# A transformer block on one core: three up-projections placed at the end of attention, the output weights as half-precision parts, two buffers for the token activations

## Chip, cores and metric

One core of a Trainium2 chip. The metric is the device time of one execution in microseconds; the profiled execution is one more execution of the same program.

## The reference

2048 tokens of 448 features. Layer norm, then 16-head attention (28 features a head), an output projection `wo` and a residual; then layer norm and a product-key expert layer (PEER): 16 heads each score 64 + 64 keys, take the best 8 of each, the best 8 of their 64 sums, a softmax over these, and of 4096 experts (`u`, `v`) sum the chosen.

```python
h = x + softmax(q @ k.T * Dh ** -0.5) @ v @ wo          # q, k, v = layernorm(x) @ wqkv, per head
xf = layernorm(h)
s1, s2 = xf @ w_q[..., :dk] @ k1.T, xf @ w_q[..., dk:] @ k2.T
i1, i2 = top8(s1), top8(s2); top_s, top_e = top8(t1[:, None] + t2[None, :])
act = gelu(einsum("nd,nhkd->nhk", xf, u[top_e]))
h2 = h + einsum("nhk,nhk,nhkd->nd", softmax(top_s), act, v[top_e])
```

## The kernel before

Every product that needs more than half precision is made from parts: `products` (L50) lists 4 + 4 + 3 matmuls of high and low parts, `mm_all` (L90) issues these 11, so that all of them carry line 92. Tokens go in four blocks `b` of 512, in tiles of 128.

**First stage (to about 160 us).** Layer norm, queries, keys and values; they go to DRAM. The weights are scaled by a power of two that a `Scale` (L130) finds: `see` takes a maximum on VectorE (DVE), `share` spreads it over the partitions with a transposition on TensorE (PE), `set` computes the scale. `values_of` (L410) writes the values with a per-partition scale `vscale`.

**Attention (L550, to about 872 us).** 256 steps `u`: 16 groups `n` (4 blocks x 4 groups of 4 heads) of 16 key tiles. In each step PE makes the scores of step u + 2 (L563), ScalarE (ACT) takes exponentials (L567), PE sums the values (L589). `load_kv` (L217) loads a piece of four key tiles, keys at L212 and values at L224, in one of four buffers, into the buffer that has just been read; so a piece is issued some 11 steps before PE first reads it. `finish` (L570) transposes and normalizes a group's output into `ob`. Beside the steps a `weave` (L174) runs generators, each with a count of steps and an interval of time in steps; whichever is due first issues next. Folding the expert queries' weights and splitting `u` and `v` run there, and for blocks 0 to 2 the output projection `project(b)` (L635), the search for the best keys `search(b)` (L753), and the pairs, partly on GpSimd (POOL, L810). `load_wo` (L622) loads `wo` and splits it into two 32-bit parts that PE reads as fp32r, on DVE (L626) and POOL (L627).

**`project`, a tile of 128 tokens:** transposes of `ob` (L121), high part on ACT or DVE, low part (L127, L128), 11 matmuls with `woh` and `wol` (L92), activation to `at` (L666), residual, moments (L711, L109, L112), norm (L115), transposes and the parts `XHb`, `XLb` in `X[b]`.

**Last projection, first weights, last scores (872 to 965 us).** `project(3)` with its own buffers, `weights(0)` (L932) and `kept_scores(3)` (L731) are woven (L1119, L1134). `weights(b)` reads the chosen slots from DRAM (`st`), makes per 16 tokens a comparison `p1` (L969) and per 32 tokens factors (L948, L954) on DVE, and sums them on PE (L996) into `G`, 32 times.

**Experts (965 us to the end).** Per block 32 slices `f`: `up` (L1141) is 11 matmuls of 512 columns and a Gelu into a ring of buffers, `weigh` (L1157) multiplies by `G` (L1163), and splits (L1164, L1165), then 12 matmuls into four sums (L1190). `ready` (L1172) sets how far `up` runs ahead: before the sums of slice f, f + 3 are made or n + (32 - n)(f + 1) // 26 if that is more, n being those made before the block; block 0 starts with n = 0. Beside block 0 a generator `later` does the rest of the pairs and all searches of block 3 on DVE, transposes slots on PE (L899) and copies them on ACT (L96); it is set to run over the first 58% of the block.

DMAs are issued from SyncE's queue (SP), which takes them in order. Lines of one engine's queue mostly follow the order written, but some that are ready earlier stand ahead of others.

Of the kernel before, what the change touches and what calls it, by code (L numbers as in the profile page):

```python
# [29 lines left out]
LS = 2.0 ** 11  # L30
TOP = 14
ONE = 2.0 ** 15
QS = 2.0 ** 2 / (XS * 2.0 ** TOP)

# [26 lines left out]
def block(ctx: ExitStack, tc: tile.TileContext, x, wqk, wv, wo, wq, k12, uT, v, cst, out):  # L61
# [20 lines left out]
    gscale = const.tile([128, 1], F32)  # L82
    vscale = const.tile([128, 1], F32)
    escale = const.tile([128, 4], F32)
# [84 lines left out]
    def times(dst, src, c):  # L169
        nc.vector.tensor_scalar(dst, src, c, None, op0=OP.mult)  # L170
# [46 lines left out]
    def load_kv(n):  # L217

        if n < len(PIECES):
            _, g, c = PIECES[n]  # L220
            kS = lp.tile([128, 2, 512], F16, name="kS", bufs=4)
            halves(kS, ks_d[g], slice(512 * c, 512 * c + 512))
            V = lp.tile([128, 4, 4, 32], F32, name="V", bufs=4)
            nc.sync.dma_start(V.rearrange("p t h d -> p (t h d)"), v_d[g, c].rearrange("p t c -> p (t c)"))  # L224
            kv[n] = kS, V

# [77 lines left out]

    US, VS, WS = Scale(0, 32), Scale(1, 32), Scale(2, H)

    fp = ExitStack()
    raw_p = fp.enter_context(tc.tile_pool(name="raw", bufs=2, reuse_waits="tile"))
    with ExitStack() as c0:
# [48 lines left out]
        def scale_wv():  # L358
            S = Scale(3, 2)
            scaled(S, wvr, [(wvh[:, 2 * i:2 * i + 2], wvl[:, 2 * i:2 * i + 2]) for i in range(2)])  # L360
            times(vscale, S.floor, 2.0 ** -TOP / XS)

# [47 lines left out]
        def values_of(b):  # L410
            for j in range(4):
                c = slice(128 * j, 128 * j + 128)
                pv = ps.tile([128, D], F32, name="pq", bufs=4)
                mm_all(pv, products(lambda t: XH[b][:, t, c], lambda t: XL[b][:, t, c],
                                    lambda t: wvh[:, t], lambda t: wvl[:, t]))
                nc.scalar.activation(vst[j][:, :, :DH], pv.rearrange("p (h d) -> p h d", h=H), AF.Identity, scale=vscale)
                (nc.scalar if b > 1 else nc.sync).dma_start(v_d[:, b, :, j].rearrange("g p c -> p g c"),
                                                                    vst[j].rearrange("p (g h) d -> p g (h d)", g=4))
# [131 lines left out]
    def attention(paired):  # L550
# [32 lines left out]
        def values(u, Pt):  # L583
            n, k = divmod(u, NT)
            if k == 0:
                O[n] = P[0].tile([128, 512], F32, name="A")
            V = kv[u // 4][1]
            for j in range(4):
                nc.tensor.matmul(O[n][32 * j:32 * j + 32], V[:, k % 4, j], Pt[:, j], start=k == 0, stop=k == NT - 1)  # L589
            if k % 4 == 3:  # L590
                load_kv(u // 4 + 4)
            if k == NT - 1:
                o = pp.tile([128, 512], F32, name="o", bufs=1)
                nc.vector.tensor_copy(o, O.pop(n))  # L594
                return o
# [11 lines left out]
        for u in range(steps):  # L607
            if u + 2 < steps:
                Pts[u + 2] = scores(u + 2)
            flush()  # L610
            if u % NT == 2 and u > NT:
                finish(u // NT - 1, done)
            if u in Pts:
                summed(u)
            if u in paired:
                summed(u + 1)
            yield
        finish(4 * NB - 1, done)
        yield


    def load_wo():  # L622
        prev = None
        for g in range(5):
            if prev:
                nc.vector.tensor_copy(woh[:, g - 1], prev)  # L626
                nc.gpsimd.tensor_tensor(wol[:, g - 1], prev, woh[:, g - 1].bitcast(F32), op=OP.subtract)  # L627
            if g < 4:
                prev = w2.tile([128, 512], F32, name="wor", tag="xt")[:, :D]
                nc.sync.dma_start(prev, wo[:, g])  # L630
            yield

    X = {}

    def project(b, offset=5, room=None):  # L635

        X[b] = XH, XL = bx.tile([128, 4, 512], F16, name="XHb"), bx.tile([128, 3, 512], F16, name="XLb")

# [3 lines left out]
        def tile_of(j):  # L642
# [59 lines left out]
    def load_X(b):  # L702
        X[b] = XH, XL = bx.tile([128, 4, 512], F16, name="XHb"), bx.tile([128, 3, 512], F16, name="XLb")
        nc.sync.dma_start(XH, x_d[b][:, :4])
        nc.sync.dma_start(XL, x_d[b][:, 4:])

    def moments(pool, xt):
# [345 lines left out]
    with tc.manual_schedule(engines={ET.PE, ET.DVE, ET.Activation, ET.Pool, ET.SP}):  # L1053
        load_kv(2)
        load_kv(3)
        begin = [67 + 4, 67 + 64, 67 + 128]
        start = [t + 26 for t in begin]
# [16 lines left out]
        for k in range(8):  # L1074
            nc.gpsimd.memset(places[:, k], float(k))
        r2 = ExitStack()
# [27 lines left out]


    us = {}

    def load_u(f):
        u = be.tile([128, 2, 4, 128], F16, name="u")
        nc.sync.dma_start(u.rearrange("p k t e -> p k (t e)"), us_d[f])  # L1110
        return u

    with tc.manual_schedule(engines={ET.PE, ET.DVE, ET.Activation, ET.Pool, ET.SP}):
        room = {"xt": [ring[4 * j + 2] for j in range(4)], "at": [ring[3], ring[7]]}
        pools = [tc.tile_pool(name="sw0", bufs=1, side="right", reuse_waits="tile")]
        with ExitStack() as c1:
            pools = [c1.enter_context(pools[0])]
            w0, sc = weights(0), kept_scores(3, pools)
            weave((project(3, 2, room), 12, 0, 0.25), (islice(w0, 1), 1, 0.01, 0.02), (islice(sc, 1), 1, 0.02, 0.03),  # L1119
                  (islice(w0, 8), 8, 0.05, 0.27), (islice(sc, 4), 4, 0.125, 0.29))  # L1120
            r2.close()
            be = ctx.enter_context(tc.tile_pool(name="be", bufs=3, reuse_waits="tile"))
            c2 = c1.enter_context(ExitStack())
# [3 lines left out]
            def loads():  # L1127
                store_X(3)
                yield
                for f in range(3):  # L1130
# [7 lines left out]
    ring += [bv.tile([128, 512], F32, name=f"ring{i}", bufs=1) for i in range(16, 20)]  # L1138
    acts = {}

    def up(b, f, name):  # L1141

        XH, XL = X[b]
        u = us.pop(f, None) or load_u(f)
        p = P[0].tile([128, 512], F32, name=name)
        mm_all(p, [(l, r) for r, l in products(lambda t: XH[:, t], lambda t: XL[:, t],
                                               lambda t: u[:, 0, t], lambda t: u[:, 1, t])])
        act = ring[f % 20] if b else ring[16 + f % 4]
        nc.scalar.activation(act, p, AF.Gelu_apprx_tanh, scale=ugelu)  # L1149
        acts[f] = act  # L1150

    def ups(b, n):
# [60 lines left out]
    for b in range(NB):  # L1213
        n = AHEAD if b else 0
        if b:
# [59 lines left out]
```

## Time and profile before

| | us |
|---|---|
| median of 3 runs | 1644.02 (1638.12 to 1646.05) |
| profiled execution | 1642.62 |
| span of its profile | 1640.8 |
| PE busy | 1560.6 (95%) |
| DVE busy | 1198.4 (73%) |
| ACT busy | 931.9 (57%) |
| POOL busy | 364.7 (22%) |

Busy time counts an instruction from its start to its end; matmuls overlap, so PE can be busy for the whole of a stretch and still not run at its peak. The granted clock is TensorE's, as a share of 2.4 GHz; 0.50 is 1.2 GHz. A row of a timeline begins with the start and the length in us; what is in brackets is the engine's idle time just before and what ended it.

### The profile page before, as it was taken

What the parts mean: (1) busy time and instruction counts of PE and PEld (TensorE: products, weight loads), DVE (VectorE), ACT (ScalarE), POOL (GpSimd) and SP (SyncE); (2) the same over time, 40 slices, a digit from 0 to 9 for tenths busy, and PEclk for the clock granted to TensorE, in tenths of its full rate; (3) what the DMA queues carried; (4) which work ended last, traced back from release to release, by engine and by line L of the source; (5) the groups of instructions that cost most, each with busy time, mean ns of one, the idle gap of its engine ahead of it and who ended that gap; (6) DMA issues with size and microseconds to landing.
All of it is one profiled execution on the core that took longest, in us unless ns stands there. A gap on an engine that the chain in (4) does not pass through costs nothing.

```text
span 1640.8 us, 33316 instructions
## 1 busy us (share of the span) xinstructions
PE 1560.6 (95%) x12585; PEld 678.9 (41%) x12585; DVE 1198.4 (73%) x3875; ACT 931.9 (57%) x1272; POOL 364.7 (22%) x488
## 2 busy tenths in 40 slices
PE   5999999999999998999988998999999999999999
PEld 3444222233333332233325654455545554555444
DVE  7762432645688677765798999959999899779832
ACT  3545778979888887888773443233423344334322
POOL 1241003555204565487524000000000000000000
PEclk9999999999999999999998999999999999999999
DMA  8424965677853475457622434444444533554454
GB/s 281 134 97 129 305 215 190 213 242 253 286 173 96 151 242 180 130 162 235 189 87 78 131 94 148 125 125 144 119 127 138 156 105 108 156 153 129 117 146 129
DMA packets 158881, 263.34 MB, mean 160 GB/s; under 512 B 14336, under 2 KB 90880, under 8 KB 158720
## 3 DMA queue, kind: packets, MB, share of 16 engines
q1 hardware_dynamic: 154496, 259.12, 50.5%
q10 hardware_dynamic: 4224, 2.10, 0.4%
q8 instruction: 98, 1.61, 0.4%
q14 instruction: 63, 0.52, 0.1%
HBM read 211.88 MB, written 49.28 MB: 159 GB/s over the span
## 4 chain that ended last, share of the span: by engine, by line
PE 63%; DVE 27%; DMA 5%; ACT 2%; issue 2%; POOL 1%; SPq 0%; DVEq 0%; POOLq 0%; ACTq 0%
PE acc L1190 14%; PE M L92 12%; PE A L589 10%; PE S L563 9%; PE A L92 7%; PE pq L92 6%; DVE p L969 4%; DVE ti L799 3%; DVE pos L826 2%; DVE G L990 2%; DVE ti L798 2%; ACT P L567 2%; DVE fg L954 2%; DMA raw<-in_uT_dram 2%; PE M L262 1%
## 5 line engine op out<-in xcount | busy, mean ns | idle before, releaser
L567 ACT ACTIVATE P<-S,escale 128x1024 f32<-128x1024 f32 x512 | 534.5, 1131 | 75.9 <-PE S L563 75.9
L1190 PE MATMUL acc<-v,w 128*128 128x448 f16 x1536 | 305.4, 352 | 0.1
L589 PE MATMUL A<-P,V 128*32 128x512 f32 x2048 | 266.0, 609 | 3.7 <-DVE o L594 3.7
L563 PE MATMUL S<-qS,kS 32*128 32x512 f16 x3072 | 240.1, 380 | 7.7 <-ACT P L567 6.0
L1190 PEld LDWEIGHTS <-w 128*128 128x128 f16 x1536 | 148.7, 98 | 141.3 <-ACT w L1164 0.9
L1164 ACT ACTIVATE w<-ring 128x512 f16<-128x512 f32 x128 | 80.5, 630 | 209.7 <-PE acc L1190 109.9
L92 PEld LDWEIGHTS <-u 128*128 128x128 f16 x1408 | 133.7, 98 | 152.5 <-issue 12.3
L969 DVE TENSOR_TENSOR p<-st,iota 128x2048 f16<-128x2048 f16 x128 | 156.0, 1219 | 7.7 <-PE A L996 4.1
L563 PEld LDWEIGHTS <-kS 32*128 32x128 f16 x3072 | 65.8, 92 | 210.6 <-issue 171.7
L92 PE MATMUL A<-XHb,u 128*128 128x512 f16 x568 | 137.8, 386 | 5.1 <-DVE G L990 3.9
L1165 DVE SCALAR_TENSOR_TENSOR w<-w,ring 128x512 f16<-128x512 f16 x128 | 87.2, 687 | 66.2 <-ACT w L1164 66.2
L92 PE MATMUL M<-w,XHb 128*128 128x512 f16 x512 | 127.9, 380 | 4.2 <-DVE ob L580 3.1
L1163 DVE SCALAR_TENSOR_TENSOR ring<-ring,wscale,G 128x512 f32<-128x512 f32 x128 | 92.7, 744 | 34.6 <-ACT ring L1149 34.5
L92 PE MATMUL M<-XHb,u 128*128 128x512 f16 x456 | 112.4, 382 | 0.8 <-DVE G L990 0.8
L1149 ACT ACTIVATE ring<-A,ugelu 128x512 f32<-128x512 f32 x71 | 48.5, 684 | 84.6 <-PE A L92 84.6
L589 PEld LDWEIGHTS A<-P,V 128*32 128x32 f32 x2048 | 45.8, 109 | 119.1 <-issue 108.3
L850 POOL TENSOR_TENSOR sel<-sel,iv 128x256 f16<-128x256 f16 x80 | 54.4, 712 | 171.6 <-DVE sel L846 171.6
L798 DVE MAX8 ti<-fresh 128x8 f32<-128x64 f32 x384 | 80.6, 210 | 16.3 <-ACT fresh L776 16.2
L1149 ACT ACTIVATE ring<-M,ugelu 128x512 f32<-128x512 f32 x57 | 39.2, 688 | 81.7 <-PE M L92 81.5
L799 DVE FIND_INDEX8 ti<-ti,fresh 128x8 uint32<-128x64 f32 x384 | 84.2, 219 | 0.0
L1026 POOL TENSOR_SCALAR raw<-raw,scale 128x512 f32<-128x512 f32 (+1 forms) x64 | 47.3, 740 | 151.8 <-PE M L262 112.2
L954 DVE TENSOR_TENSOR fg<-f,st 128x2048 f16<-128x2048 f16 x64 | 78.0, 1218 | 0.1
(197 smaller groups left out, 2130.4 us busy)
## 6 DMA issues: line engine op xcount, KB each, us to landing
v<-vs SPq DMA_DIRECT2D x128, 336.0 KB, 2.9
u<-us SPq DMA_DIRECT2D x128, 256.0 KB, 2.6
w<-wp SPq DMA_DIRECT2D x56, 512.0 KB, 5.9
kS<-ks SPq DMA_DIRECT2D x64, 256.0 KB, 4.5
V<-vd SPq DMA_DIRECT2D x64, 256.0 KB, 2.8
raw<-in_uT_dram SPq DMA_DIRECT2D x64, 256.0 KB, 5.3
wr<-in_wq_dram SPq DMA_DIRECT2D x32, 448.0 KB, 4.3
raw<-in_v_dram SPq DMA_DIRECT2D x64, 224.0 KB, 5.1
```

The source lines that it names most:

```text
L92: nc.tensor.matmul(ps, l, r, start=i == 0, stop=i == len(pairs) - 1)
L563: nc.tensor.matmul(S[j // 2][:, j % 2], kS[r, a, 128 * (k % 4):128 * (k % 4) + 128], qS[r, c], start=m == 0, stop=m == 2)
L567: nc.scalar.activation(Pt[:, 2 * i:2 * i + 2], S[i], AF.Exp, scale=escale[:, n % 4:n % 4 + 1])
L589: nc.tensor.matmul(O[n][32 * j:32 * j + 32], V[:, k % 4, j], Pt[:, j], start=k == 0, stop=k == NT - 1)
L798: nc.vector.max(t8[:, 4 * i + k], src[:, 64 * k:64 * k + 64])
L799: nc.vector.max_index(i8[:, 4 * i + k], t8[:, 4 * i + k], src[:, 64 * k:64 * k + 64])
L954: nc.vector.tensor_tensor(fg.rearrange("p t k f u -> p t k (f u)"), f1.rearrange("p t f u -> p t (f u)").unsqueeze(2).to_broadcast([128, T ...
L969: newest[0] = nc.vector.tensor_tensor(p1, pairs(0, s, TG, 128), ids(TG, 128), op=OP.is_equal).ins
L1149: nc.scalar.activation(act, p, AF.Gelu_apprx_tanh, scale=ugelu)
L1163: nc.vector.scalar_tensor_tensor(av, av, wscale, of_expert(b, f), op0=OP.mult, op1=OP.mult)
L1165: nc.vector.scalar_tensor_tensor(w[:, 1], w[:, 0], -LS, a, op0=OP.mult, op1=OP.add)
L1190: nc.tensor.matmul(acc[j][:, :D], l, r, start=f == 0 and k == 0, stop=f == 31 and k == 2)
```

## The change

- `wo` is scaled by a power of two (`WO`, a `Scale`) and split into two fp16 parts, both on DVE; the attention's output is split into fp16 parts too. The values carry a fixed scale `VS1` instead of `vscale`, and a pointer scale `pscale` after the projection makes up for both. The first project starts two steps later (67 + 6 instead of 67 + 4), the search of block 2 ends two steps earlier.
- Keys and values have three buffers instead of four, a piece is issued some 7 steps before PE first reads it.
- `XHb` and `XLb` have two buffers. `X[0]`, the first three `u` slices and the slots of `weights(0)` are loaded in the last steps of the attention.
- Block 0's first three up-projections run early: `up(0, 0)` before the attention's last `finish`, in a buffer of the scores; `up(0, 1)` and `up(0, 2)` at the head of the next stage. Block 0 then starts with three made.
- The first step of `weights(0)` on DVE stands at the head of that stage, before `project(3)`.

The diff, cut to its core (`up`, `load_u` and the pool `be` move up in the file unchanged but for `p`):

```diff
-            kS = lp.tile([128, 2, 512], F16, name="kS", bufs=4)
+            kS = lp.tile([128, 2, 512], F16, name="kS", bufs=3)
...
-            V = lp.tile([128, 4, 4, 32], F32, name="V", bufs=4)
+            V = lp.tile([128, 4, 4, 32], F32, name="V", bufs=3)
...
-                nc.scalar.activation(vst[j][:, :, :DH], pv.rearrange("p (h d) -> p h d", h=H), AF.Identity, scale=vscale)
+                nc.scalar.activation(vst[j][:, :, :DH], pv.rearrange("p (h d) -> p h d", h=H), AF.Copy, scale=VS1)
...
-                load_kv(u // 4 + 4)
+                load_kv(u // 4 + 3)
...
+        up(0, 0, None, pss.tile([128, 2, 512], F32, name="S")[:, 0])
         finish(4 * NB - 1, done)
...
     def load_wo():
...
-                nc.vector.tensor_copy(woh[:, g - 1], prev)
-                nc.gpsimd.tensor_tensor(wol[:, g - 1], prev, woh[:, g - 1].bitcast(F32), op=OP.subtract)
...
+        for g, r in enumerate(raws):
+            nc.sync.dma_start(r, wo[:, g])
+        yield
+        yield
+        for g, r in enumerate(raws):
+            WO.see(g, r)
+            if g == 1:
+                yield
+        yield from WO.share()
+        yield
+        for g, r in enumerate(raws):
+            times(woh[:, g], r, WO.scale)
+            nc.vector.scalar_tensor_tensor(wol[:, g], r, WO.scale, woh[:, g], op0=OP.mult, op1=OP.subtract)
+            if g == 1:
+                yield
+        nc.vector.tensor_scalar(pscale, WO.floor, VW.floor, 2.0 ** (-TOP - 4), op0=OP.mult, op1=OP.mult)
...
-            oh = w2.tile([128, 4, 128], FR, name="oh2", bufs=1)
-            ol = w2.tile([128, 3, 128], FR, name="ol2", bufs=1)
+            oh = w2.tile([128, 4, 128], F16, name="oh2", bufs=1)
+            ol = w2.tile([128, 3, 128], F16, name="ol2", bufs=1)
...
-            nc.scalar.activation(at, pa[:, :D], AF.Copy)
+            nc.scalar.activation(at, pa[:, :D], AF.Identity, scale=pscale)
...
-        begin = [67 + 4, 67 + 64, 67 + 128]
+        begin = [67 + 6, 67 + 64, 67 + 128]
...
-        woh = wo_p.tile([128, 4, D], FR)
-        wol = wo_p.tile([128, 4, D], FR)
-        work = [(a, 257 - FOLDED, 0, 257 - FOLDED), (load_wo(), 5, 0, 5)]
+        woh = wo_p.tile([128, 4, D], F16)
+        wol = wo_p.tile([128, 4, D], F16)
+        work = [(a, 257 - FOLDED, 0, 257 - FOLDED), (load_wo(), 9, 0, 6.5)]
...
-            work += [(look, SEARCH, t, t + SEARCH)]
+            work += [(look, SEARCH, t, t + SEARCH - 2 * (b == 2))]
...
+        def first_loads():
+            load_X(0)
+            for f in range(3):
+                us[f] = load_u(f)
+                yield
+            next(w0)
+            yield
+
+        w0 = weights(0)
+        work += [(first_loads(), 5, 174, 184)]
...
-            w0, sc = weights(0), kept_scores(3, pools)
-            weave((project(3, 2, room), 12, 0, 0.25), (islice(w0, 1), 1, 0.01, 0.02), (islice(sc, 1), 1, 0.02, 0.03),
-                  (islice(w0, 8), 8, 0.05, 0.27), (islice(sc, 4), 4, 0.125, 0.29))
+            sc = kept_scores(3, pools)
+            def first_up(f):
+                up(0, f, "A")
+                yield
+
+            weave((first_up(1), 1, 0, 0), (islice(w0, 1), 1, 0, 0.002), (project(3, 2, room), 12, 0, 0.25), (first_up(2), 1, 0.012, 0.012), (islice(sc, 1), 1, 0.02, 0.03),
+                  (islice(w0, 7), 7, 0.05, 0.27), (islice(sc, 4), 4, 0.125, 0.29))
...
-            load_X(0)
...
-        n = AHEAD if b else 0
+        n = AHEAD if b else UP0
```

## Rows read from the trace of the kernel before

**Rows 1.** Stages: length, busy us of each engine (instructions), granted clock, DMA share, GB/s

```profile
335.00:870.00 535.00, 517.26 (x4611) 171.48 (x4605) 383.70 (x1905) 444.06 (x479) 264.41 (x355) 0.99 0.57 182
870.00:905.00 35.00, 27.28 (x232) 19.94 (x231) 27.59 (x57) 9.25 (x16) 16.61 (x24) 0.80 0.33 106
905.00:965.00 60.00, 56.77 (x1040) 37.98 (x1039) 55.73 (x58) 25.50 (x43) 0.22 (x1) 0.99 0.35 109
965.00:1062.00 97.00, 91.67 (x471) 44.13 (x468) 97.00 (x579) 31.02 (x51) 0.00 (x0) 0.97 0.45 133
1062.00:1131.00 69.00, 67.21 (x497) 35.69 (x496) 45.78 (x69) 24.45 (x51) 0.00 (x0) 1.00 0.45 135
```

The engines stand in the order PE, PEld (its weight loads), DVE, ACT, POOL.

**Rows 2.** The same view, five microseconds each, in the last projection

```profile
885.00:890.00 5.00, 2.29 (x42) 1.68 (x40) 4.32 (x9) 2.09 (x4) 1.85 (x3) 0.85 0.32 97
890.00:895.00 5.00, 4.45 (x11) 3.51 (x11) 4.82 (x7) 0.96 (x2) 0.01 (x1) 0.50 0.09 35
```

**Rows 3.** Timeline of PE: a projection with 32-bit parts, and what follows

```profile
366.90 1.08 PE L92 MATMUL M<-woh,oh 128*128 128x448 f32 x4
...
369.33 0.83 PE L563 MATMUL S<-qS,kS 32*128 32x512 f16 x12
```

**Rows 4.** Timeline of PE: two successive groups of the values projection

```profile
141.89 0.92 PE L92 MATMUL pq<-wvh,XH 128*128 128x448 f16 x4
...
143.97 0.92 PE L92 MATMUL pq<-wvh,XH 128*128 128x448 f16 x4
```

**Rows 5.** Timeline of DVE: the weights of slice 14 in block 0

```profile
1044.84 0.68 DVE L1165 SCALAR_TENSOR_TENSOR w<-w,ring 128x512 f16<-128x512 f16 x1
```

**Rows 6.** Waits of PE in block 0: total us, times, longest

```profile
PE M L899 <- ACT st L96: 5.2, 1, 5.2
```

**Rows 7.** Groups of instructions by line and form: busy us, mean ns

```profile
L416 ACT ACTIVATE vst<-pq,vscale 128x448 f32<-128x448 f32 x16 | 10.2, 635 | 19.9 <-PE pq L92 18.4 <-issue 1.4
L666 ACT ACTIVATE at<-M 128x448 f32<-128x448 f32 x12 | 6.5, 544 | 14.3 <-PE M L92 14.3
L1149 ACT ACT_TABLE_LOAD x3 | 3.8, 1283 | 0.1
```

**Rows 8.** Timeline of SP: the load of the 20th piece of keys

```profile
329.03 0.49 SPq L212 DMA_DIRECT2D kS<-ks  x1
```

**Rows 9.** Timeline of PE: the first scores that read this piece

```profile
351.77 1.08 PE L563 MATMUL S<-qS,kS 32*128 32x512 f16 x12
```

**Rows 10.** DMA issues: count, KB each, median us from issue to landing

```profile
kS<-ks SPq DMA_DIRECT2D x64, 256.0 KB, 4.5
```

**Rows 11.** Timeline of PE: the second and third up-projection and the first sum

```profile
968.61 1.89 PE L92 MATMUL A<-XHb,u 128*128 128x512 f16 x8
...
970.99 1.89 PE L92 MATMUL A<-XHb,u 128*128 128x512 f16 x8
...
973.36 2.73 PE L1190 MATMUL acc<-v,w 128*128 128x448 f16 x12
```

**Rows 12.** The chain that ended last: one of two equal projection groups

```profile
876.46 4.46 PE M L92 x11
```

**Rows 13.** Timeline of PE: the attention's last transposes

```profile
872.68 0.66 PE L577 MATMUL M<-ct,o 128*128 128x128 f32 x4 [1.34 <-DVE o L594]
```

**Rows 14.** Waits of DVE from 868 to 965 us

```profile
DVE f L948 <- DMA st<-sd: 2.0, 1, 2.0
DVE ring L668 <- ACT ring L666: 2.0, 1, 2.0
DVE ol L127 <- ACT oh L651: 1.2, 1, 1.2
```

**Rows 15.** Timeline of DVE: the first factors and comparison of the first weights

```profile
878.31 0.74 DVE L948 TENSOR_TENSOR f<-st,iota 128x1024 f16<-128x1024 f16 x1 [2.00 <-DMA st<-sd]
...
880.23 1.31 DVE L969 TENSOR_TENSOR p<-st,iota 128x2048 f16<-128x2048 f16 x1
```

**Rows 16.** Timeline of PE: the sums of slice 14 in block 0

```profile
1048.76 2.43 PE L1190 MATMUL acc<-v,w 128*128 128x448 f16 x12
```

More of the change, by code (lines that the diff above doesn't have):

```diff
@@ L31 @@
 TOP = 14
+UP0 = 3
 ONE = 2.0 ** 15
+VS1 = 2.0 ** 4 / (XS * 2.0 ** TOP)
 QS = 2.0 ** 2 / (XS * 2.0 ** TOP)
@@ L82, in block @@
     gscale = const.tile([128, 1], F32)
-    vscale = const.tile([128, 1], F32)
+    pscale = const.tile([128, 1], F32)
     escale = const.tile([128, 4], F32)
@@ L303, in parts @@
                 nc.sync.dma_start(wp_d[h // 4][:, :, h % 4].rearrange("p f t c -> p f (t c)"), hl)
-    US, VS, WS = Scale(0, 32), Scale(1, 32), Scale(2, H)
+    US, VS, WS, VW, WO = Scale(0, 32), Scale(1, 32), Scale(2, H), Scale(3, 2, 60), Scale(8, 4, 60)
     fp = ExitStack()
@@ L358, in scale_wv @@
         def scale_wv():
-            S = Scale(3, 2)
-            scaled(S, wvr, [(wvh[:, 2 * i:2 * i + 2], wvl[:, 2 * i:2 * i + 2]) for i in range(2)])
-            times(vscale, S.floor, 2.0 ** -TOP / XS)
+            scaled(VW, wvr, [(wvh[:, 2 * i:2 * i + 2], wvl[:, 2 * i:2 * i + 2]) for i in range(2)])
         def scale_wqk(g):
@@ L622, in load_wo @@
     def load_wo():
-        prev = None
-        for g in range(5):
-            if prev:
-                nc.vector.tensor_copy(woh[:, g - 1], prev)
-                nc.gpsimd.tensor_tensor(wol[:, g - 1], prev, woh[:, g - 1].bitcast(F32), op=OP.subtract)
[L628 to L631, printed above, removed]
+        raws = [w2.tile([128, 512], F32, name="wor", tag="xt")[:, :D] for _ in range(2)]
+        raws += [w2.tile([128, 4, 128], F32, name=n, bufs=1).rearrange("p t c -> p (t c)")[:, :D] for n in ("of", "xf")]
+        for g, r in enumerate(raws):
[15 more added lines that the diff above has]
+        yield
     X = {}
     def project(b, offset=5, room=None):
-        X[b] = XH, XL = bx.tile([128, 4, 512], F16, name="XHb"), bx.tile([128, 3, 512], F16, name="XLb")
+        X[b] = XH, XL = bx.tile([128, 4, 512], F16, name="XHb", bufs=2), bx.tile([128, 3, 512], F16, name="XLb", bufs=2)
         def place(j, name, tag, bufs):
@@ L702, in load_X, with load_u, up @@
     def load_X(b):
-        X[b] = XH, XL = bx.tile([128, 4, 512], F16, name="XHb"), bx.tile([128, 3, 512], F16, name="XLb")
+        X[b] = XH, XL = bx.tile([128, 4, 512], F16, name="XHb", bufs=2), bx.tile([128, 3, 512], F16, name="XLb", bufs=2)
         nc.sync.dma_start(XH, x_d[b][:, :4])
         nc.sync.dma_start(XL, x_d[b][:, 4:])
+    us, acts = {}, {}
+    def load_u(f):
+        u = be.tile([128, 2, 4, 128], F16, name="u")
+        nc.sync.dma_start(u.rearrange("p k t e -> p k (t e)"), us_d[f])
+        return u
+    def up(b, f, name, p=None):
+        XH, XL = X[b]
+        u = us.pop(f, None) or load_u(f)
+        if p is None:
+            p = P[0].tile([128, 512], F32, name=name)
+        mm_all(p, [(l, r) for r, l in products(lambda t: XH[:, t], lambda t: XL[:, t],
+                                               lambda t: u[:, 0, t], lambda t: u[:, 1, t])])
+        act = ring[f % 20] if b else spare[f % 4]
+        nc.scalar.activation(act, p, AF.Gelu_apprx_tanh, scale=ugelu)
+        acts[f] = act
     def moments(pool, xt):
@@ L1054, in block @@
         load_kv(2)
-        load_kv(3)
-        begin = [67 + 4, 67 + 64, 67 + 128]
+        begin = [67 + 6, 67 + 64, 67 + 128]
         start = [t + 26 for t in begin]
@@ L1075, in block @@
             nc.gpsimd.memset(places[:, k], float(k))
+        be = ctx.enter_context(tc.tile_pool(name="be", bufs=3, reuse_waits="tile"))
+        spare = [be.tile([128, 512], F32, name=f"ring{i}", bufs=1) for i in range(16, 19)]
         r2 = ExitStack()
@@ L1103, in block @@
     ring = [gp.tile([128, 512], F32, name=f"ring{i}") for i in range(16)]
[L1106 to L1111, printed above, removed]
     with tc.manual_schedule(engines={ET.PE, ET.DVE, ET.Activation, ET.Pool, ET.SP}):
@@ L1117, in block @@
             pools = [c1.enter_context(pools[0])]
-            w0, sc = weights(0), kept_scores(3, pools)
-            weave((project(3, 2, room), 12, 0, 0.25), (islice(w0, 1), 1, 0.01, 0.02), (islice(sc, 1), 1, 0.02, 0.03),
-                  (islice(w0, 8), 8, 0.05, 0.27), (islice(sc, 4), 4, 0.125, 0.29))
+            sc = kept_scores(3, pools)
+            def first_up(f):
+                up(0, f, "A")
+                yield
+            weave((first_up(1), 1, 0, 0), (islice(w0, 1), 1, 0, 0.002), (project(3, 2, room), 12, 0, 0.25), (first_up(2), 1, 0.012, 0.012), (islice(sc, 1), 1, 0.02, 0.03),
+                  (islice(w0, 7), 7, 0.05, 0.27), (islice(sc, 4), 4, 0.125, 0.29))
             r2.close()
-            be = ctx.enter_context(tc.tile_pool(name="be", bufs=3, reuse_waits="tile"))
             c2 = c1.enter_context(ExitStack())
@@ L1129, in loads @@
                 yield
-                for f in range(3):
+                for f in range(UP0, UP0 + 3):
                     us[f] = load_u(f)
@@ L1134, in block @@
             weave((w0, WEIGHTS - 9, 0.29, 1), (sc, 13, 0.29, 0.92), (loads(), 4, 0.6, 0.8))
-            load_X(0)
     bv = ctx.enter_context(tc.tile_pool(name="bv", bufs=3, reuse_waits="tile"))
     gw = ctx.enter_context(tc.tile_pool(name="gw", bufs=2, side="right", reuse_waits="tile"))
[L1138 to L1150, printed above, removed]
+    spare.append(bv.tile([128, 512], F32, name="ring19", bufs=1))
+    ring += spare
     def ups(b, n):
```

## The prediction

> **What bounds the kernel now.** I read the stages first, then who waits in each, then single stretches in order of time. The stages [rows 1] show three regimes. From 335 to 870 us (the attention's main part) the TensorE (PE) is busy 517 of 535 us and the VectorE (DVE) 384: PE sets the pace, with ScalarE (ACT, 444) close behind. From 870 to 965 us (the last projection, the first weights and the last scores) neither engine is full: PE 27.3 of 35 and 56.8 of 60, DVE 27.6 of 35 and 55.7 of 60. So this stretch is a chain between them, and PE also loses time to its clock: the granted clock is 0.80 there, and 0.50, the 1.2 GHz level, from 890 to 895 us, after five microseconds with PE busy for only 2.29 [rows 1, 2]. From 965 to 1062 us, the first two thirds of block 0 of the experts, DVE is busy 97.00 of 97 us and PE 91.7; from 1062 to 1131 us PE has 67.2 of 69 and DVE only 45.8. Block 0 is thus bound by both, one after the other. The later blocks run after 1131 us; the change doesn't touch their work, and I give them nothing.
>
> **The change, part by part.**
>
> *Half-precision output weights in attention.* A projection multiplies 11 pairs of 448 columns. With the 32-bit parts, a group takes 369.33 - 366.90 = 2.43 us from its first matmul to the next work [rows 3]. The same 11 x 448 columns with half-precision parts, in the values projection at full clock, take 143.97 - 141.89 = 2.08 us [rows 4]. That is 0.35 us less for each of 12 tiles that run inside the attention, 4.2 us. PE is the bound there, so I count it whole; the bounds are 0 (ACT takes over between projections) and 4.2.
>
> By the Trainium skill's "TensorE: Matmul & The Clock Gate", section "Back-to-back issue gap", a matmul's spacing is its columns over 2.4 GHz plus 2.5 ns, 189 ns for 448 columns whatever the type: by that the old group would take 2.08 us too, and the 4.2 us would be 0. The trace shows 221 ns (2.43 us over 11), so I go by the row; the other outcome is rival 3.
>
> *Loading wo.* Before: four casts on DVE, four subtractions on POOL. After: four reductions, a transposition of the maximum on PE, a few one-column operations, then eight scaling operations on DVE, near 0.7 us each by the nearest row [rows 5], so some 6 us more DVE work. DVE is idle 28% of this stage [rows 1], so this work is free; without that cover it would cost those 6 us. Not free is PE's wait for the transposition's input: behind it in PE's queue stand the scores of the next step, and ACT waits for these. The first project starts two steps later, and the search after it runs into the next one by a step, both inside filled PE time. Nearest rows for the wait: nothing, and 5.2 us, the longest wait of PE for a transposition that I found [rows 6]. I take 1.0, nearer to nothing because DVE is not full here.
>
> *Scale as a pointer.* The activation after a projection changes from an immediate to a pointer scale and the one after the values the other way: 544 against 635 ns [rows 7], 0.09 us for each of 16 tiles. In attention ACT's idle sixth hides it, and in the last projection it is 0.4 us of a chain, which I leave in the range; the 16 values activations gain as much where PE is ahead. Both 0.
>
> *Three buffers for keys and values instead of four.* A piece is then issued four steps later. The 20th piece's load was issued at 329.03 us, first used at 351.77, and a load lands in 4.5 us [rows 8, 9, 10]: 22.7 us of lead, the shortest that I found among the pieces after the start. Four steps are some 8 to 12 us, so over 10 us are left and 4.5 needed. Cost 0; if SyncE's queue stood still for more than 6 us, PE would wait the rest. The new loads in that queue (two for X, three for u, one for the slots, six issues) go out in the last ten steps, after the last keys. Two X buffers alone buy nothing: no wait for X appears; they let X[0] be resident while X[3] is made.
>
> *The end of the attention.* Three up-projections move here. One costs 970.99 - 968.61 = 2.38 us of PE [rows 11], 7.1 us in all. PE gets back 2 x (4.46 - 2.08) = 4.8 us, as two of the four projection groups ran at the low clock at 4.46 us [rows 12] and the first up-projection fills the 1.34 us that PE waited for the last sums [rows 13] and keeps it busy; with 0.6 us for the other two groups PE has 1.7 us more work in a stretch with 10.9 us idle [rows 1]. Of DVE's waits, 2.0 us for the slots' DMA and 1.2 us before the first low part [rows 14] can go: the slots are now loaded in attention, and the first factors (881.54 - 878.31 = 3.2 us of DVE [rows 15]) can run while the transposes do. Against it, up(0) holds PE until about 870.9 + 2.4 = 873.3 us, 0.6 us past the start of the last transposes at 872.68 [rows 13]. Its activation needs a table load of 1.28 us [rows 7] which is hidden by ACT's idle time, 25.8 of 35 us [rows 1]. Together 3.2 - 0.6, I take 2.5 us; the bounds are -8.5 (rival 4) and 9.3, when the ring wait of 2.0 us [rows 14] and the 4.8 us of low clock go from the path as well.
>
> *The start of block 0.* PE started with three up-projections before its first sum at 973.36 us [rows 11]; they are gone, 7.1 us. But DVE is full until 1062 us [rows 1], and its work there is unchanged: a PE that comes earlier waits for weights. How far DVE leads is seen where the lead is short: the weights of slice 14 were ready at 1044.84 + 0.68 = 1045.5 us, and PE used them at 1048.76 us [rows 5, 16]. So by DVE alone PE may come 3.2 us earlier there. By the new shares one of the three saved up-projections falls after that point (29 over 26 steps instead of 32), where PE is the bound: 3.2 + 2.4 = 5.6 us at most by this slice. PE's wait of 5.2 us for slots [rows 6], near slice 8, is paced by DVE too and will keep its place; behind it two of the three are still saved, 4.8 us. I take 4.8; the bounds are 0 and 12.3 (all three and the wait of 5.2).
>
> By the same page, same section, its sustained spacing of 131 ns for 512 columns would make an up-projection 1.44 us, and this term 2.9 us as an estimate. The rows show 216 ns, so I keep 4.8.
>
> **The sum.** 4.2 - 1.0 + 2.5 + 4.8 = 10.5 us less. The profiled execution took 1642.6 us (span 1640.8 and 1.8 around it), which makes 1632.1; the median of the runs is 1.4 us above it, so 1633.5 us.
>
> **Rivals.**
> 1. *DVE keeps block 0.* Its 97.00 of 97 us speak for it; that PE, too, had only 5.3 us idle speaks against. The three are paid and nothing comes back in block 0: 3.2 + 2.5 = 5.7 us, 1638.3.
> 2. *DVE's order yields.* If the weights are taken first, because their activations are ready, and the searches slide into the 23 us of DVE idle time after 1062 us, the whole 7.1 us and the 5.2 us wait come back: 3.2 + 2.5 + 12.3 = 18 us, 1626.0. For it speaks that the first three activations are there before the weights end; against it that the searches are queued between the weights of one slice and the next.
> 3. *The half-precision group is no faster* than the 32-bit one at full clock: 4.2 us less gain, 1637.7. Against it stand the two rows; the page's rule above is what speaks for it.
> 4. *Slower: the early up-projections stand in front of the last projection.* PE takes its queue in order. If up(1) and up(2) are issued when the transposes of the last projection are already ready, these wait 2 x 2.38, plus the 0.6, and DVE's first factors, 3.2, stand before the first low part: up to 8.5 us on a chain of four tiles that pass through PE, ACT, DVE and POOL in turn. With block 0 held by DVE as in rival 1, nothing returns: 8.5 - 3.2 = 5.3 us more, 1649.3. From 3.2 us of delay on it makes the kernel slower. Against it: 10.9 us of PE idle in the stretch.
>
> **How the numbers follow.** Forecast 0.42, rival 1 0.20, rival 2 0.20, rival 3 0.08, rival 4 0.10. A measurement of this kernel can tell about 0.5% (8.2 us) from no change, so faster means below 1635.8 us. The forecast gives 0.35 of its 0.42 to faster, rival 2 all of its 0.20, rival 1 0.03 and rival 3 0.01; that is 0.59. Same: 0.07 + 0.17 + 0.07 and 0.05 of rival 4, 0.36. Slower: the other 0.05 of rival 4, which its 1649.3 us passes when the wo wait comes to its bound as well. The range reaches from 1623, rival 2 with 3 us more at the attention's end, to 1641.5, rival 1 with a wo wait of about 4 us; it leaves out rival 4 and the tails.
>
> **What would show it.** In the changed profile the 11-matmul groups in attention should stand 2.08 us apart from the next work, all four in the last projection too, with no granted clock near 0.5 from 874 to 895 us. From the last transposes of the attention to block 0's first sum, 973.36 - 872.68 = 100.7 us before [rows 11, 13], it should be some 93 us, though three up-projections are now made by then. Block 0's first sum should follow the weights by one up-projection, not three, and the block should end about 10 us earlier. I am wrong if PE's waits for DVE in block 0 grow by the 7 us, if the last projection's tiles start later by more than 3 us, or if waits for key loads appear.

## The result, and the profile after

The changed kernel takes 1648.62 us (median of 22 runs), the kernel before beside it 1643.55; the ratio is 1.0034, with a 95% interval of 1.0025 to 1.0043. The change costs 5.1 us where I forecast a gain of 10.5. The profiled execution spans 1647.4 us against 1640.8, at a mean clock of 0.988.

The stages of the changed kernel, cut 11 us later than in [rows 1], the last one at block 0's end as there (same columns):

```profile
335.00:881.00 546.00, 519.98 (x4620) 160.70 (x4614) 397.75 (x1933) 446.60 (x481) 261.43 (x351) 0.99 0.59 188
881.00:916.00 35.00, 30.12 (x260) 16.95 (x255) 28.07 (x42) 12.26 (x20) 15.20 (x22) 0.90 0.11 34
916.00:976.00 60.00, 57.88 (x1052) 38.54 (x1050) 55.62 (x59) 25.76 (x43) 0.74 (x2) 0.99 0.36 115
976.00:1073.00 97.00, 89.91 (x448) 42.63 (x444) 94.62 (x576) 30.08 (x50) 0.00 (x0) 0.95 0.44 132
1073.00:1136.00 63.00, 62.53 (x458) 33.17 (x457) 45.97 (x70) 20.60 (x43) 0.00 (x0) 1.00 0.46 134
```

By these cuts attention takes 11 us more for 2.7 us more of PE work: PE was idle 17.7 us of 535 before and is idle 26.0 of 546 now. The end of attention is no shorter, though three up-projections are made there and the granted clock is higher (0.90 for 0.80). Block 0's last stage is 6 us shorter. The starts of the attention's scores tell where the 11 us are: step 222 comes within a microsecond of where it came before, step 250 13.0 us later, the last values 10.7 us later. That is the search of block 2.

In the timeline of PE before, two steps of attention in this stretch run in 5.85 us (758.81 to 764.66); `S` are the tiles of the scores, `P` the exponentials that ACT makes of them:

```profile
758.81 1.92 PE L589 MATMUL A<-P,V 128*32 128x512 f32 x16
760.67 0.83 PE L563 MATMUL S<-qS,kS 32*128 32x512 f16 x12
761.42 1.04 PE L92 MATMUL M<-w,XHb 128*128 128x512 f16 x4
762.30 0.81 PE L92 MATMUL M<-w,XLb 128*128 128x512 f16 x3
762.95 1.03 PE L92 MATMUL M<-w,XHb 128*128 128x512 f16 x4
763.91 0.83 PE L563 MATMUL S<-qS,kS 32*128 32x512 f16 x12
764.66 1.92 PE L589 MATMUL A<-P,V 128*32 128x512 f32 x16
```

and after in 7.17 us (759.24 to 766.41):

```profile
759.24 1.92 PE L589 MATMUL A<-P,V 128*32 128x512 f32 x16
761.09 1.04 PE L94 MATMUL M<-w,XHb 128*128 128x512 f16 x4
761.97 0.81 PE L94 MATMUL M<-w,XLb 128*128 128x512 f16 x3
762.61 1.03 PE L94 MATMUL M<-w,XHb 128*128 128x512 f16 x4
763.57 1.04 PE L563 MATMUL S<-qS,kS 32*128 32x512 f16 x14
765.66 0.82 PE L563 MATMUL S<-qS,kS 32*128 32x512 f16 x10 [1.05 <-ACT P L567]
766.41 1.92 PE L589 MATMUL A<-P,V 128*32 128x512 f32 x16
```

The instructions are the same, in another order. Before, the search's 11 matmuls (on `w`) stand between the scores of two steps; after, they stand ahead of both, and the scores follow back to back. A step's scores fill two tiles of `S` and there are three, so the fourth tile waits 1.05 us for ACT. ACT meanwhile has had nothing to do while the search's matmuls ran, as its timeline after shows:

```profile
763.68 0.60 ACT L806 ACTIVATE fresh<-M 128x512 f32<-128x512 f32 x1 [2.23 <-PE M L94]
764.50 4.13 ACT L567 ACTIVATE P<-S,escale 128x1024 f32<-128x1024 f32 x4 [0.22 <-PE S L563]
```

The two largest waits of PE between 755 and 885 us after (total us, times, longest):

```profile
PE S L563 <- ACT P L567: 8.4, 8, 1.1
PE M L929 <- ACT fresh L806: 3.8, 1, 3.8
```

Before, the first of these was 0.6 us, once:

```profile
PE S L563 <- ACT P L567: 0.6, 1, 0.6
```

The planner, `weave`, explains the order. Thirty-three items over 33 steps have the same due times as the steps (both at a half), and the attention, first in the list, is issued first. Over 31 steps the first item is due at 0.47, so the search goes ahead of its step. The items are 0.94 steps apart, so after eight pairs of steps the search is a whole step ahead and its matmuls stand between the scores again: from step 240 on a pair takes 5.85 us, and PE waits eight times.

The rest of the trace after: a projection's group of 11 in attention stands 2.18 us before the next scores, 0.25 less than in [rows 3] and not 0.35:

```profile
360.92 0.93 PE L94 MATMUL M<-woh,oh 128*128 128x448 f16 x4
...
363.10 0.83 PE L563 MATMUL S<-qS,kS 32*128 32x512 f16 x12
```

And block 0's first sum follows one up-projection instead of three, against [rows 11]:

```profile
976.35 3.01 PE L94 MATMUL A<-XHb,u 128*128 128x512 f16 x8
979.19 0.81 PE L94 MATMUL A<-XLb,u 128*128 128x512 f16 x3
979.84 0.59 PE L94 MATMUL A<-XHb,u 128*128 128x512 f16 x2
980.27 2.43 PE L1213 MATMUL acc<-v,w 128*128 128x448 f16 x12
```

From the last values to that sum it is 98.6 us, against 102.4 before.

### The profile page after: what moved, and what is told of

Its sections match the earlier page's. It is cut to its first block, busy times and chain, and to the rows that moved or that the text cites. A ratio compares the mean times of both kernels' runs of the same rounds, so it can differ in the third digit from the quotient of the medians.

```text
span 1647.4 us, 33307 instructions
## 1 busy us (share of the span) xinstructions
PE 1560.5 (95%) x12586; PEld 661.4 (40%) x12586; DVE 1211.5 (74%) x3889; ACT 931.3 (57%) x1272; POOL 359.8 (22%) x484
## 4 chain that ended last, share of the span: by engine, by line
PE 68%; DVE 23%; ACT 3%; DMA 3%; issue 2%; SPq 0%; POOL 0%; DVEq 0%; POOLq 0%; ACTq 0%
PE acc L1213 14%; PE M L94 12%; PE A L589 12%; PE S L563 11%; PE A L94 7%; PE pq L94 6%; DVE p L999 4%; ACT P L567 3%; DVE ti L829 2%; DVE G L1020 2%; DVE fg L984 2%; PE M L264 1%; DVE ti L828 1%; PE A L1026 1%; DVE f L978 1%
```

## The experiments

The theory was that the order of the planner makes the loss (A). Against it stood crowding (B: the same items in fewer steps cost more in any order), and the early up-projections, buffers or wo loading (C). Ratios are to the kernel before on the same chip.

**1. The search of block 2 at its full length.**

```diff
-            work += [(look, SEARCH, t, t + SEARCH - 2 * (b == 2))]
+            work += [(look, SEARCH, t, t + SEARCH)]
```

> The changed kernel with the search of block 2 spread over 33 steps of attention again instead of 31; all else stays. Theory A (order): with 33 items over 33 steps the search's items and the attention's steps have equal due times, and the step's scores are issued ahead of the search's matmuls; with 31 the search's matmuls come first, two steps' scores then stand one behind the other, and each of eight pairs of steps pays 7.18 instead of 5.86 us. It expects about 10 us less than the changed kernel, 1638 to 1639 us, with steps 222 to 238 taking about 47 us instead of 57. Theory B (crowding: the same items in fewer steps cost more whatever their order) expects the same 10 us here. Theory C (the early up-projections, the three buffers or the wo loading make the loss, and the stretch of the search only passes it on) expects 1646 to 1649 us.

Measured: 1639.76 us, ratio 0.9984 (0.9971 to 0.9998). Against the changed kernel's 1.0034 that is 0.5%, 8.2 us (7.4 with the same kernel measured again, run 10). Steps 222 to 238 take 49.2 us against 60.1, and PE's wait for `P` is back at 0.6 us. C falls.

**2. The short search alone, in the kernel before.** The reverse edit.

> The kernel before with one edit, the search of block 2 over 31 steps instead of 33. Theories A and B expect about 10 us more than before, 1652 to 1655 us, lost between steps 222 and 238. Theory C expects no change beyond 2 us.

Measured: 1653.3 us, ratio 1.0068 (1.0044 to 1.0091), 10.1 us above the 1643.16 beside it. Its waits have the row of the changed kernel, number for number:

```profile
PE S L563 <- ACT P L567: 8.4, 8, 1.1
```

**3. The full length, a tenth of a step earlier.**

```diff
-            work += [(look, SEARCH, t, t + SEARCH - 2 * (b == 2))]
+            work += [(look, SEARCH, t - 0.1 * (b == 2), t + SEARCH - 0.1 * (b == 2))]
```

> The changed kernel with the search of block 2 over its full 33 steps, but begun a tenth of a step earlier, so that each of its items is issued just ahead of the attention step that it shared its due time with. Theory A (order) expects the loss without any shortening, and in all sixteen pairs of steps instead of eight: 16 x 1.3 = 21 us over the kernel with the full search, about 1659 us. Theory B (crowding) expects the time of the full search, about 1638 us.

Measured: 1645.68 us in a single execution (span 1643.4). The largest of its waits of PE from 755 to 885 us:

```profile
PE S L563 <- ACT P L567: 15.9, 16, 1.1
```

The mechanism is as A said: 16 waits, with no shortening, so B falls. The size is not: 7.0 us of span over experiment 1, not 21. Step 250 comes 15.9 us later than there, but the last values only 12.1, since a wait of 7.2 us for ScalarE's `fresh` is gone from the list (experiment 8), and the stretch to block 0's first sum is 95.7 us instead of 100.3, with 3.4 us of it at the low clock instead of 13.7 (experiment 9).

**4. No early up-projections, on experiment 1.** The first three `u` are still loaded in attention, and so not again beside the first weights.

```diff
-UP0 = 3
+UP0 = 0
...
-        up(0, 0, None, pss.tile([128, 2, 512], F32, name="S")[:, 0])
...
-            weave((first_up(1), 1, 0, 0), (islice(w0, 1), 1, 0, 0.002), (project(3, 2, room), 12, 0, 0.25), (first_up(2), 1, 0.012, 0.012), (islice(sc, 1), 1, 0.02, 0.03),
+            weave((islice(w0, 1), 1, 0, 0.002), (project(3, 2, room), 12, 0, 0.25), (islice(sc, 1), 1, 0.02, 0.03),
```

> The kernel with the full search and without the early up-projections: all 32 of block 0 are made in block 0 again, three of them ahead of its first sum; the loads of X and u stay in attention. If the early up-projections gain what the traces show (the stretch from the last values to block 0's first sum 3.9 us shorter, nothing at the end of attention), it takes 4 us more than the kernel with the full search, about 1643 us. By the prediction's terms (2.5 at the end of attention and 4.8 in block 0) it is 7.3 us more, 1646 us. If they only move work, no change.

Measured: 1644.21 us, 4.45 above experiment 1 beside it. From the last values to block 0's last sum the traces have 259.7 us without and 255.6 with the early up-projections, 4.1 us. They gain, but a good half of my 7.3, and part of that is the clock's: between the last values and block 0's first sum 20.5 us are at the low clock without them, 13.7 with them. And the first projection starts as late without them as with them, 9.0 us after the last values, as the timeline of PE without them shows; before the change it was 5.5:

```profile
871.22 1.54 PE L123 MATMUL M<-ct,ob 128*128 128x128 f32 x6 [1.01 <-DVE ob L580]
876.27 1.65 PE L94 MATMUL M<-woh,oh 128*128 128x448 f16 x4 [3.51 <-DVE oh L130]
```

PE waits 3.51 us there for a low part, because in DVE's timeline the first factors stand ahead of it:

```profile
871.08 1.22 DVE L983 TENSOR_TENSOR fg<-f,st 128x2048 f16<-128x2048 f16 x1
872.21 3.14 DVE L998 TENSOR_TENSOR p<-st,iota 128x2048 f16<-128x2048 f16 x1
875.27 0.54 DVE L129 TENSOR_TENSOR ol<-M,oh 128x384 f16<-128x384 f32 x1
```

**5. up(1) and up(2) behind the transposes, on experiment 1.**

```diff
-            weave((first_up(1), 1, 0, 0), (islice(w0, 1), 1, 0, 0.002), (project(3, 2, room), 12, 0, 0.25), (first_up(2), 1, 0.012, 0.012), (islice(sc, 1), 1, 0.02, 0.03),
+            weave((first_up(1), 1, 0.012, 0.012), (islice(w0, 1), 1, 0, 0.002), (project(3, 2, room), 12, 0, 0.25), (first_up(2), 1, 0.054, 0.054), (islice(sc, 1), 1, 0.02, 0.03),
```

> The kernel with the full search, with up(1) and up(2) issued behind the transposes of the last projection's first and the first multiplication after the second tile instead of in front of them. If the place of the two up-projections in PE's queue sets the end of attention (the mechanism of rival 4), the first tile's transposes start 1.7 us earlier (they wait for ob alone, ready at 3.9 us after the last values instead of 5.7) and the stretch from the last values to block 0's first sum is 1 to 3 us shorter than the 100.4 us with the full search. If the stretch is paced by the VectorE, whose first p takes 3.15 us in front of the first low part, it stays within 1 us.

Measured: 1637.1 us in a single execution; the stretch is 96.8 us, 3.5 shorter. But the first projection still starts 9.2 us after the last values, so the reason expected isn't the one that acted (experiment 9).

**6. Half-precision wo alone, in the kernel before:** its loading, scaling, types, the pointer scale and the start of the first project, nothing else of the change.

> The kernel before with half-precision parts of wo alone (its loading and scaling, the pointer scale, the first project two steps later); four buffers for keys and values, no early up-projections, the search as before. By the prediction's terms (4.2 in attention, 1.0 for the loading) it is 3.2 us faster than before, about 1640 us. By what the two traces show (0.24 us for a tile instead of 0.35, and the search of block 0 running into the second project for a step, 1.8 us) it is 1 us faster, 1642 us. By rival 3 (half precision no faster) it is 1 us slower, 1644 us.

Measured: 1643.61 us, ratio 0.9995 (0.9982 to 1.0009), that is 3.0 us less to 1.5 more. The 3.2 of the prediction lies just outside; between 1 us less and 1 us more it can't tell.

**7. The second project a step later, on experiment 1** (`begin = [67 + 6, 67 + 65, 67 + 128]`).

> The kernel with the full search, with the second project and the search behind it one step later, so that the search of block 0 has ended when the second project begins. If the step in which both run costs what the trace of the changed kernel showed there (1.8 us around step 130, where two groups of 11 matmuls stand in one step), the stretch from step 130 to step 160 is 1 to 2 us shorter; if the matmuls cost the same wherever they stand, it is unchanged within 0.3 us.

Measured: 1641.8 us in a single execution; steps 130 to 160 take 78.2 us against 78.0. A miss: what I took for the cost of an overlap was moved work. Steps 160 to 195 take 112.1 us against 106.7; PE waits 5.2 us there for DVE's `ob`, which it doesn't in experiment 1. Why stays open.

**8. A third buffer for `fresh`, on experiment 1.**

```diff
-            src = sp.tile([128, 512], F32, name="fresh")
+            src = sp.tile([128, 512], F32, name="fresh", bufs=3)
```

> The kernel with the full search, with three buffers instead of two for the scores that the search hands from ScalarE to VectorE. Theory D (buffers): PE's wait of 6.5 us at the end of attention, for an activation that waits 6.1 us for the VectorE to free one of the two buffers, goes, and attention ends 4 to 6.5 us earlier, 1634 to 1636 us in all. Theory E (the VectorE is full there): the wait is only passed on, to a later activation or to the copy of the last sums, and the time stays at 1638 to 1640 us.

Measured: 1640.43 us, ratio 0.9983 (0.9972 to 0.9994): theory E. The largest wait of PE with two buffers, then two of those with three:

```profile
PE M L929 <- ACT fresh L806: 7.2, 2, 6.5
```

```profile
PE M L577 <- DVE o L594: 7.2, 1, 7.2
PE M L929 <- ACT fresh L806: 1.4, 2, 0.7
```

The 7.2 us move from the buffer to the copy of the last sums: DVE is full at the end of attention. This is also why a loss of PE's there comes back in part: in the changed kernel the wait for `fresh` is 3.8 us, with the full search 7.2.

**9, 10. Experiment 5 timed, and experiment 1 again, on one chip.**

> The kernel of the run with up(1) and up(2) behind the transposes, now timed, beside the kernel with the full search on the same chip. Its one profile had no stretch at the low clock between 860 and 963 us, where that of the full search had 10.2 us of it. If the place of the two up-projections was worth the 3.6 us, it is 3 to 4 us faster than the full search beside it; if that was the clock of a single execution, the two agree within 1 us, since the first projection still started 9.2 us after the last values.

> The kernel with the full search once more, as the base for the two others of this call: 1638 to 1640 us by its first five rounds.

Measured: 1637.57 us, ratio 0.9964 (0.9950 to 0.9977), and 1641.09 us, ratio 0.9989 (0.9976 to 1.0002). So the edit makes the kernel 3.5 us faster, with intervals that just touch. The stretch repeats itself: 96.8 us twice (5, 9), 100.3 and 100.2 (1, 10). The windows (us, then busy time by engine, clock, DMA share, GB/s), first of experiment 1, then of 9, then of 7, which has both up-projections in front as experiment 1 has, and its last values 4.9 us later:

```profile
885.00:890.00 5.00, 2.95 (x73) 2.62 (x72) 4.20 (x6) 2.42 (x5) 0.61 (x2) 1.00 0.19 51
890.00:895.00 5.00, 3.29 (x11) 1.33 (x10) 3.97 (x8) 0.17 (x1) 0.74 (x2) 0.58 0.29 92
895.00:900.00 5.00, 4.28 (x14) 1.81 (x13) 3.52 (x8) 1.83 (x3) 0.74 (x2) 0.50 0.13 46
```

```profile
885.00:890.00 5.00, 4.27 (x69) 2.99 (x66) 3.90 (x6) 2.51 (x6) 0.82 (x3) 1.00 0.18 57
890.00:895.00 5.00, 3.40 (x42) 1.90 (x38) 4.68 (x9) 2.13 (x4) 0.74 (x2) 1.00 0.31 95
```

```profile
890.00:895.00 5.00, 2.97 (x73) 2.48 (x72) 4.00 (x6) 2.43 (x5) 0.76 (x2) 1.00 0.20 54
895.00:900.00 5.00, 2.63 (x15) 1.13 (x13) 4.68 (x9) 1.50 (x3) 0.75 (x2) 1.00 0.30 92
900.00:905.00 5.00, 4.93 (x54) 3.04 (x55) 4.81 (x9) 1.81 (x4) 0.74 (x2) 1.00 0.13 46
```

In experiment 1 PE is busy for only 2.95 us from 885 to 890, and then the clock falls to 1.2 GHz for 10.2 us, over the third tile's projection. With up(2) held back PE is busy for 4.27 us there and the clock stays at 2.4. But in run 7, with experiment 1's order in PE's queue, PE is busy for 2.97 us and then 2.63, and the clock stays as well. Its stretch is 96.8 us too, as short as run 9's (run 3, also with both in front and no low clock in the last projection, has 95.7). So the 3.5 us between these profiles go with the clock; by run 7, a single execution, the place as such gains nothing in the stretch.

The timed runs agree: the three runs of 10 with a mean clock of 0.989 or 0.990 take 1637.3 to 1638.0 us, the five of 9, all at 0.988 to 0.990, 1637.1 to 1638.5. That the edit keeps the clock up more often is likely from the medians. Why the clock fell in experiment 1 and not in run 7 isn't shown.

**11. The first factors behind the first low parts, on experiment 1** (`(islice(w0, 1), 1, 0.035, 0.045)`).

> The kernel with the full search, with the first factors of the weights (f, fg, p on the VectorE) behind the first tile's low parts instead of in front of them. Without the early up-projections the first projection started 9.0 us after the last values all the same, against 5.5 us before the change, so theory F says that the factors hold it, p at 3.15 us above all: with them behind, it starts 5.5 to 6.5 us after the last values, and the stretch to block 0's first sum is 1 to 3 us shorter, 1637 us. If the VectorE's sum of work paces the stretch whatever its order, the projection starts earlier but the stretch stays within 1 us, 1639 us.

Measured: 1639.11 us, ratio 0.9977 (0.9966 to 0.9988). The first projection starts at 8.9 us all the same: theory F fails as put.

**12. GpSimd's pairs of block 2 end five steps earlier, on experiment 1** (`252 - FOLDED` for `257 - FOLDED`).

> The kernel with the full search, with GpSimd's pairs of block 2 spread to end five steps earlier. In the full search GpSimd still works on them until 884 us, and the first p took 3.15 us there against 1.31 us in the kernel before; f took 2.42 against 0.74 us. If the work of GpSimd beside them is what makes them long, p is back at 1.2 to 1.5 us and the first projection starts 2 us sooner; the time is then 1636 to 1638 us. If their length has another reason, p stays at 3 us. The VectorE's share of the pairs comes earlier too, so PE's wait of 6.5 us for it can grow by 1 to 3 us.

Measured: 1641.31 us, ratio 0.9987 (0.9977 to 0.9997). GpSimd is done at 873.7 us, and DVE's `p`, 3.15 us in experiment 1, takes 1.22:

```profile
877.38 1.22 DVE L999 TENSOR_TENSOR p<-st,iota 128x2048 f16<-128x2048 f16 x1
879.49 0.56 DVE L129 TENSOR_TENSOR ol<-M,oh 128x384 f16<-128x384 f32 x1 [0.90 <-ACT oh L662]
```

But the first projection still starts at 8.9 us, and attention takes 2.5 us longer from step 222 to the last values (117.2 us against 114.8).

**13, 14. Both holds taken away.** Run 13 joins the edits of 5 and 11, run 14 those of 5 and 12.

> The full search with both moves: up(1) and up(2) behind the transposes, and the first factors behind the first tile's low parts. Theory G (two things hold the first projection at the same place, PE's two up-projections and the VectorE's factors, and each hides the other): with both behind, it starts 5.5 to 7 us after the last values, where either alone left it at 8.9 to 9.2. If that start matters, the stretch to block 0's first sum is 1 to 3 us below the 96.8 us of the ups behind alone and the time 1635 to 1637 us; if only the low clock mattered, the stretch stays at 96 to 98 us without low clock and the time at 1637 to 1638 us. If the start stays near 9 us, theory G falls.

> The full search with the ups behind the transposes and GpSimd's pairs of block 2 ending five steps earlier; the factors stay in front of the low parts. p takes 1.2 us as it did with the pairs earlier alone, so by theory G the first projection starts about 2 us earlier than the 9.2 us of the ups behind alone, near 7 us after the last values. The attention itself ends 1.5 to 2 us later, as it did with the pairs earlier alone, so no gain in all: 1637 to 1639 us. If the start stays near 9 us, something else on the chain holds it.

Measured: 1639.72 us, ratio 0.9976 (0.9965 to 0.9987), and 1636.85 us, ratio 0.9961 (0.9948 to 0.9975). The first projection starts 7.0 and 7.1 us after the last values. That is theory G: PE's two up-projections and DVE's factors each hold it at 9, and either one alone hides the other. PE in run 14, with no wait left ahead of the projection:

```profile
878.24 1.89 PE L94 MATMUL A<-XHb,u 128*128 128x512 f16 x8
879.97 0.81 PE L94 MATMUL A<-XLb,u 128*128 128x512 f16 x3
880.62 0.60 PE L123 MATMUL M<-ct,ob 128*128 128x128 f32 x4
881.10 0.92 PE L94 MATMUL M<-woh,oh 128*128 128x448 f16 x4
```

The stretch to block 0's first sum is then 98.0 us in run 13, with 6.8 us of it at the low clock, and 94.0 in run 14, with 3.4. Run 9 has 96.8 with the same 3.4, so the shorter `p` and the earlier start are worth 2.8 us of the stretch in run 14. The attention gives it back: from step 222 to the last values it takes 117.2 us there, as in run 12, and 114.4 in run 9, so that the times of runs 9 and 14 can't be told apart. In run 13 the last values come 2.6 us later than in run 9 (873.1 against 870.5), but step 222, ahead of both edits, comes 2.9 us later already. Runs 9 and 14 are faster than both kernels, by 0.36% and 0.39% of the kernel before.

## Why the prediction was wrong

**The step that failed** is a term that the prediction put at nothing without a reason: the shorter search of block 2, `SEARCH - 2 * (b == 2)`. It is named among the changes, and the sum has no term for it. The nearest sentence, under "Loading wo", is about another search, that of block 0, which "runs into the next one by a step, both inside filled PE time"; there it held (run 7). Such a sentence asks only how full PE is. The planner's spans are also an order, and a tie in due time was holding that order up: with it gone, PE waits eight times for a tile of scores. The shorter search costs 10.1 us alone in the kernel before (run 2) and 8.2 in the changed one (run 1), more than all the rest of the change gains. The row to read was in the trace of before: in its search stretch scores and search alternate, and PE waits for `P` only once, for 0.6 us.

**Rival 4's time was right and its cause wrong.** It gave 1649.3 us, from up-projections ahead of the last projection and with block 0 giving nothing back. That the time agrees is luck. They do stand in the way, but together with the factors: the last projection starts 9.8 us after the last values, 4.3 later than before, which was one of the prediction's signs of being wrong. Yet the stretch to block 0's first sum is 3.8 us shorter, and block 0's gain is there. Without the search the change is a small gain at most (0.9984 in run 1; 0.9989 in run 10, whose interval reaches no change).

**Half-precision wo, 4.2 us less 1.0.** The mechanism was right, the size off: 0.25 us for a tile (2.18 against 2.43), so 12 x 0.25 = 3.0 for the 4.2. I had taken the 2.08 us of a group that is followed by another group [rows 4]; followed by scores it takes 0.10 us longer. With the loading, run 6 leaves 0.2 us (between 3.0 less and 1.5 more). The wait for the loading's transposition, put at 1.0, is 1.4 us in the changed kernel, 0.7 in run 1 and 2.0 in run 6, so this term was right. Rival 3 is refuted for the group itself and can't be told from the forecast for the kernel.

**The end of attention, 2.5 us: nothing.** From the last values to the last sums of the first weights it is 94.8 us before and after. The waits for the slots went as predicted, and the factors came earlier: the first `p` starts 6.7 us after the last values, 9.3 before. But earlier means in front of the first low part and beside GpSimd's work, and the up-projections in PE's queue hold the same place. The clock's part came by half: of two stretches of 6.8 us at 1.2 GHz over the four groups one is left, over the third tile.

**Block 0, 4.8 us:** from those last sums to block 0's last one it took 163.5 us before and takes 159.4 after, 4.1 less. This was nearly right. DVE did not keep it (rival 1): PE's waits in block 0 come to 7.5 us, against 6.6 before. The searches did slide a little, as rival 2 has it: the last of them starts 93.2 us after those sums, 87.6 before. But 4.1 came back and not its 12.3.

**Buffers and pointer scale, 0:** no wait of PE for keys or values appears after, and the 0.09 us of the pointer changed sides as read (634 ns for the projection's activation, 544 for the values'). With wo, the earlier loads and the factors' place they make 0.8 us more (run 4's ratio of 1.0005, 0.9990 to 1.0020), that is nothing that can be told.

**The sum as measured**, by ratios: 8.2 for the search (run 1), -3.5 for the early up-projections (run 4 against run 1; -4.45 by medians) and 0.8 for the rest (run 4) make 5.5 us more, against 5.6 for the ratio of 1.0034. These are steps of one chain of kernels, so they must add up, and each carries some 3 us of noise.

## What to carry over

In a schedule woven from due times, work out for each changed span which of two neighbours is now issued first, ties above all: the order inside a step cost more here than the density. Where two queues hold the same start, taking either away shows nothing; take away both before calling a theory wrong. And before a difference between two profiles is put down to an edit, compare stretches with the same granted clock: what looked like the price of a place was the clock's (runs 1, 7 and 9).

## What was not expected of the hardware

The same VectorE comparison, `p` (128x2048, 16 bit), takes 1.22 us with GpSimd idle (run 12) and 3.15 us beside GpSimd's additions. These take longer too: the first two, of 1024 and 512 columns, 3.03 and 2.02 us, against 2.12 and 1.16 in run 12. In experiment 1, DVE and then GpSimd:

```profile
874.21 1.21 DVE L984 TENSOR_TENSOR fg<-f,st 128x2048 f16<-128x2048 f16 x1
875.35 3.15 DVE L999 TENSOR_TENSOR p<-st,iota 128x2048 f16<-128x2048 f16 x1
```

```profile
874.38 3.03 POOL L884 TENSOR_TENSOR sel<-sel 128x1024 f16<-128x1024 f16 x1
877.49 2.02 POOL L884 TENSOR_TENSOR sel<-sel 128x512 f16<-128x512 f16 x1
```

The Trainium skill's "SBUF — State Buffer", section "SBUF: two separate sides", says that a VectorE operation with two inputs in SBUF and a GpSimd operation that reads SBUF exclude each other for a whole instruction, the later one waiting. The trace agrees: the four end in turn, `fg` at 875.43, the first addition at 877.41, `p` at 878.50, the second addition at 879.51. From one end to the next that leaves 1.98, 1.09 and 1.02 us, near the 2.12, 1.22 and 1.16 that they take in run 12.
